# Segment-recurrent attention beside a gated MLP on one core: work of GpSimd given to VectorE and ScalarE, and a new order of all tasks

## The chip, the cores and the metric

The kernel runs on one core of one Trainium2 chip. A core has five engines that run side by side and meet only at semaphores: TensorE (PE, matrix multiplication into the accumulation memory PSUM), VectorE (DVE), ScalarE (ACT), GpSimd (POOL) and SyncE (SP, which here only issues transfers). The metric is the device time of one execution in microseconds, as the median of several runs. Beside it there is one profiled execution, with a record for each instruction; its span runs from the first to the last record.

## The reference

Input is one sequence x of 2048 tokens by 512 features, in bf16. Two branches are computed and mixed token by token:

```python
g = sigmoid((x * gate_w).sum(-1))            # one number per token
a = attention(x, wq, wk, wv, wo, beta)       # branch A
h = gelu(x @ w_gate) * (x @ w_up)            # branch B, 1792 wide
b = h @ w_down
out = g * a + (1 - g) * b
```

Branch A has 32 heads of width 16 and works in four segments of 512 tokens. Inside a segment it is causal softmax attention. What came before enters through a memory per head, a 16x16 matrix M and a vector z:

```python
pq = phi(qs)                                 # phi(t) = t + 1 if t > 0, else exp(t)
a_mem = (pq @ M) / (pq @ z + 1e-6)
o = sigmoid(beta) * a_mem + (1 - sigmoid(beta)) * softmax(qs ks^T / 4 + mask) @ vs
pk = phi(ks);  M = M + pk^T @ vs;  z = z + pk.sum over tokens
```

## The kernel before

**An order written out by hand.** The kernel does not loop over its stages in the order in which they run. It first declares 1,364 tasks (class `Task`, `Sched.add`), each with a function that emits a few instructions, and then `Sched.run` goes through one long string, `ORDER`, word by word, and emits each task's instructions. Each engine executes its own instructions strictly in that order. A word is a task's name, then where needed `@A`, `@D`, `@P` or `@S` (the engine that takes it: ScalarE, VectorE, GpSimd or SyncE; without it the first engine of the task's list), then `#` and letters that name the buffers it takes. So the string decides the order on each engine, the engine of many small tasks, and which buffer is used again when.

**The tasks of a segment s** (c is one of four chunks of eight heads, pr a pair of chunks, kt and qt a quarter of the segment's 512 tokens, hs one of 14 pieces of the MLP's width):

- `qs.c`, `ks.c`, `vs.kt` are projections, four accumulation steps each, into one PSUM bank ("gen", two of them, letters a and b). `eq`, `ek`, `ev` move the result to SBUF on VectorE or ScalarE.
- `kes.c` and `kos.c` (function `odd_copy`) copy k times a 0/1 column, `even` or `odd`, into kO, so that both heads of a 32-row strip can be taken apart.
- `lgN`, N from 0 to 71, 18 in each segment, holds a block of logits in two of the three double banks "lg" (letters a, b, c). Before the first one, matmuls use the whole array; after it, every matmul is split into four on 32-column groups (`mm4`), and logits use four 32-row groups.
- `exNa`, `exNb` are the exponentials of the two halves, 128x1024 each, on ScalarE; `asNa`, `asNb` zero the masked part on GpSimd (`affine_select`; every ninth slot, "as8", has 64-partition pieces, two a half).
- `pvs.ce`, `pvs.co` (function `pv_group`) multiply the even and odd heads' probabilities with v: 40 matmuls of 64 to 256 columns, whose sequence is that of the list `parts`. `epv` transposes the result on VectorE, and `r`, `rg`, `n`, `m`, `o` normalise, mix with the memory's part and transpose back.
- `E`, `Q`, `Em`, `ph` (function `phi`) compute phi as min(exp(t), 1) + max(t, 0): an exponential on ScalarE, a maximum, a minimum, and an addition. `pks.pr` transposes phi(k) by two DMAs from SP, `Ms.pr` and `eM` add to the memory, `mbd` and `zbd` lay it out, `num`, `den`, `nm`, `rma`, `rmr`, `rmg` read it for the next segment. `bdec` and `wosc` scale a mask and w_o by values of sigmoid(beta), once.
- `gts.hp` and `egt` are the MLP's gate and its gelu (into one lg double bank, on ScalarE), `ups.hs` and `eup` the up projection and the product on VectorE. Going from an exponential to a gelu or back, `act` adds a tiny operation, before which a table load stands.
- `dns.qt.hs` and `wos.qt.c` add both branches' outputs into one bank; `os` scales by 1 - g, `st` stores.
- `zs.kt` reduce x * gate_w, from rows of x that lie in the place of w_down (tile wdn) and w_o until they are done; `zsp` and `g2` finish g. On SP, `lx2`, `lx3` load x of segments 2 and 3 by four DMA transpositions each, `wdn0` to `wdn3` load w_down over the rows that are done, `wo` loads w_o.

A PSUM bank may be written again only when its evacuation is done, so each TensorE task waits for the evacuation of the task two places earlier in the same set of banks, unless that was done long before.

**Lines that the steps touch.** L385 is the split matmul (L381 the undivided one), L683 logits, L743 pv, L858 M; L233 all exponentials and gelus, L231 the tiny operation and its table load; L237 and L239 copies on ScalarE and VectorE; L413 ko, L423 and L425 ke; L556 z; L610 the up product; L622 one step of `eb`; L715 and L710 masks; L760 the pv transposition; L783 m; L810, L813, L817 the maximum, minimum and addition of phi; L958 nm; L1000 and L998 os.

Of the kernel before, what the change touches and what calls it, by code (L numbers as in the profile page):

```python
# [36 lines left out]
k0f1.0 xt0.1 xt1.1 xt2.1 ext0.1 xt3.1 ext1.1 k0f2.0 ext2.1 ext3.1 k0f3.0 k0f0.1 k0f1.1 k0f2.1  # L37
k0f3.1 q0.0#ba ek0.3@A ek0.2@D ek0.1@A ek0.0@D gt0.0#b Ek0.1#a ke0.0@D#a ko0.0@D ke0.2@D#b ke0.3@D
ko0.2@D gt0.1#a Qk0.1#a eq0.0@D egt0.0#a Emk0.1 phk0.1@P#a q0.1#a egt0.1#b lg0#cb eq0.1@D v0.3#b
ko0.1@D q0.2#ab ev0.3@D Ek0.0#a gt0.5#a eq0.2@D ex0a#a Qk0.0#a ke0.1@D ex0b#b as0a gt1.4#c as0b  # L40
gt0.3#b egt0.5#c lx3 gt0.2#a egt0.3#d egt1.4#e q1.0#bc egt0.2#f up0.7#a eq1.0@D lg1#bc eup0.7
v0.1#b z0.1 ex1b#c v0.0#a z1.1 ev0.1@A z1.2 as1b lg2#ac ex1a#d q1.1#b ev0.0@D ex2b#e v0.2#a
eq1.1@D ex2a#f as2b lg3#bc ev0.2@D up0.3#b pk0.1#a tb ex3b#g up1.8#a eup0.3 ex3a#h as1a lg4#ac
eup1.8 v1.0#b as2a ex4b#i up0.11#a ev1.0@D vh0.0@A lg5#bc eup0.11 as4b k1.0#bc ex5b#j z1.3
pv0.0e#aa omg ex4a#k gt0.6#c Emk0.0 phk0.0@D#a ex5a#a vh0.1@D pk0.0#b Eq1.0#a as5a gt1.1#a epv0.0e
as3a ek1.0@D as4a as3b gt0.4#b z1.0 egt0.6#g Qq1.0#a wdn1 Emq1.0 egt1.1#h lx2 eb phq1.0@P#a
pv0.0o#a up0.13#b egt0.4#i epv0.0o lg6#ca eup0.13 k1.1#a bde0@P bde3@D z0.0 M0.0#b ex6b#b gt1.5#b
eM0.0 z3.2 ex6a#c ek1.1@D as6b M0.1#b Ek1.0#a as6a lg7#ac eM0.1 z0.2 v1.1#a ex7a#d z2.2 v1.2#b
z2.0 ex7b#g gt1.2#a bde1@D Emk1.0 z0.3 z2.3 wdn0 gt1.3#c z3.1 egt1.5#j z3.3 ev1.1@A z3.0 gt1.6#b
egt1.3#k z2.1 ev1.2@D wdn2 zsp2 egt1.2#l zbd0 up0.5#a egt1.6#m as5b up1.11#b eup0.5 pv0.1e#ab  # L50
eup1.11 lg8#ca ko0.3@D up0.10#b epv0.1e ex8a#h Qk1.0#a up0.1#a ke1.0@A#a eup0.10 as8a ex8b#i as7a
lg9#bc eup0.1 as7b up1.2#b ex9a#k as8b zsp1 pv0.1o#a ex9b#a eup1.2 lg10#ab epv0.1o q0.3#b ex10a#b
r0.0#a phk1.0@D#a up1.9#a eq0.3@A as10a r0.1#b pk1.0#b ex10b#c zsp0 lg11#ca eup1.9 v1.3#b ex11a#j
mbd0.0 zsp3 up0.0#a ev1.3@D ex11b#d as11a lg12#bc wo eup0.0 g2 q1.2#ba wdn3 ex12b#e q1.3#a eq1.2@D
ex12a#f as9b lg13#ac as10b eq1.3@D up0.6#b as9a ex13b#g as11b up1.3#a ex13a#h eup0.6 lg14#bc
eup1.3 Eq1.1#a gt2.2#a mbd0.1 ke1.1@D ex14b#i Qq1.1#a Emq1.1 phq1.1@D#b k2.0#ba rg0.1 den1#aa
gt1.0#c eden1 egt2.2#n ek2.0@D rma1.0#a bde2@D up1.10#a wos1@D egt1.0#o n0.1#a as12a up0.8#b
eup1.10 as13b rma1.1 pv0.2e#ab eup0.8 lg15#ac ex14a#a epv0.2e up2.4#b as12b rma1.2 ex15a#b up1.0#a
eup2.4 ex15b#c lg16#ba eup1.0 as13a up0.4#b rma1.3 ex16b#k pv0.2o#a eup0.4 lg17#ca ex16a#e epv0.2o
ko1.0@P k1.2#bb rmr1 ex17a#f num1.1#aa gt2.0#b r0.2#b as14a ek1.2@A rg0.2 as15a enum1.1 ex17b#g  # L60
as16a rmg1 rg0.0 gt2.3#c n0.2#b nm1.1@P#a as14b egt2.0#p gt2.1#a as17a as15b egt2.3#q as17b as16b
pv0.3e#bb egt2.1#r k1.3#a epv0.3e ke1.2@D#b lg18#bc ek1.3@D up0.2#b ex18b#h up1.1#a eup0.2 ex18a#a
ko1.1@D lg19#ac mbd0.3 up0.12#b eup1.1 ex19b#b as18a pv0.3o#a as18b eup0.12 ex19a#c lg20#bc wos2@D
epv0.3o up1.5#b ex20b#i up0.9#a eup1.5 ex20a#d ko1.3@D lg21#ac mbd0.2 up1.12#b eup0.9 ex21b#e
as20a r0.3#b v2.3#a ex21a#f eup1.12 lg22#bc ev2.3@D up2.5#b ex22a#g as20b up1.6#a ex22b#j eup2.5
o0.1 lg23#ab Ek1.1#a gt2.4#c eup1.6 as22b as21b ex23a#k Qk1.1#a as22a o0.2 as19b up2.2#b n0.0#a
as21a rg0.3 num1.0#aa gt2.6#a as19a vh1.1@D egt2.4#s vh1.0@A omz gt2.5#c enum1.0 egt2.6#t eup2.2
pv1.0e#aa n0.3#b egt2.5#u q2.0#bb Emk1.1 epv1.0e phk1.1@P#a lg24#ac eq2.0@D pv1.0o#a up1.4#b
ex24b#a epv1.0o r1.0#a nm1.0@P#b pk1.1#a q2.1#a ke1.3@A eup1.4 ex24a#b as23a num1.2#ba eq2.1@D
ex23b#c lg25#ca enum1.2 up1.13#a ex25b#h o0.0 as23b k2.1#b nm1.2@P#c eup1.13 ex25a#e wos0@D  # L70
lg26#ba up1.7#a ek2.1@D ex26a#f as25a as24a M1.0#b as25b eup1.7 ex26b#g lg27#cb as24b eM1.0 as26a
M1.1#a rg1.0 ex27b#j pv1.1e#bb as26b eM1.1 ko1.2@D wos3@P pv1.1o#a epv1.1e ex27a#a lg28#ab epv1.1o
up2.13#b ex28b#b as27a k2.2#ac as27b eup2.13 ex28a#c as28b n1.0#a lg29#cb ek2.2@A up2.3#b mbd1.1
ex29a#k up2.7#a eup2.3 ex29b#d as29a lg30#ac eup2.7 up2.8#b ex30b#e o0.3 zbd1 ex30a#f lg31#bc
as29b eup2.8 up2.10#a ex31b#g r1.1#b v2.2#b eup2.10 ex31a#h lg32#ac ev2.2@D as28a up2.0#a ex32a#i
as30b as30a pv1.2e#ba eup2.0 as31b Eq2.0#a as31a lg33#ba epv1.2e q3.0#ac m1.0@P ex32b#a k2.3#b
eq3.0@D ex33b#b as32b rg1.1 Qq2.0#a up2.1#a ex33a#c ek2.3@D as33b as32a lg34#ca eup2.1 pv1.2o#b
# [6 lines left out]
ex36b#d dn0.0.2 dn0.0.3 dn0.0.4 wo0.3.3 dn0.0.5 lg39#ac as36b dn0.0.6 os0.3@D#a ex39a#e dn0.0.7
as37b dn0.0.8 dn0.0.9 dn0.0.10 ex39b#f dn0.0.11 as39a dn0.0.12 num1.3#ba as37a dn0.0.13 wo0.0.0
enum1.3 as38b vh2.0@A wo0.0.1 wo0.0.2 wo0.0.3 o1.0 lg40#ba os0.0@A#b q2.2#ba n1.2#a ex40b#g st0.0
q2.3#a eq2.2@A Qq3.0#a phq3.0@D#a lg41#ca eq2.3@A pv2.0e#ba r1.3#b Eq2.1#a m1.2@D dn0.2.0#a
dn0.2.1 rg1.3 dn0.2.2 nm1.3@D#b dn0.2.3 ex40a#j dn0.2.4 dn0.2.5 mbd1.3 dn0.2.6 Qq2.1#a dn0.2.7
epv2.0e dn0.2.8 ex41b#k dn0.2.9 as40a dn0.2.10 o1.2 dn0.2.11 dn0.2.12 ex41a#a dn0.2.13 Emq2.1
# [1004 lines left out]
```

## Time and profile before

| quantity | value |
|---|---|
| median of 3 runs | 270.41 us (269.59 to 271.2) |
| the profiled execution's own time | 270.36 us |
| its span | 268.6 us |
| granted TensorE clock | 1.00 |
| VectorE busy | 182.7 us, 68% |
| ScalarE busy | 222.0 us, 83% |
| GpSimd busy | 142.7 us, 53% |
| exponentials L233 | 144 x 1029 ns, 137.7 us busy |
| table loads L231 | 20 x 1283 ns, 25.7 us |
| GpSimd additions of phi L817 | 4, 2128 and 2137 ns |
| the same on VectorE | 8, 676 and 730 ns |
| ko L413 | 2 on GpSimd, 1565 ns; 14 on VectorE, 403 ns |
| Q L810 on VectorE | 12, 419 and 449 ns |
| E L233 on ScalarE | 12, about 1058 ns |

The busy time of an engine is the time in which at least one of its records is open; records that follow each other overlap by some 0.1 us, so sums of the mean durations are larger. A matmul's record lasts longer than the time that it keeps the array (379 ns for 512 columns), and records of up to four column groups run side by side, so TensorE's pace is read from the distance between starts, not from a record's length. "Idle before" names what ended an engine's wait. The chain of waits goes back from the last instruction to whatever released each step; its pieces are given as start, length and what ran.

### The profile page before, as it was taken

Reading aid. Unit: us, or ns where it says so; the run is one execution under the profiler, and the core shown is the slowest. Engines: PE = TensorE matmul, PEld = TensorE weight load, DVE = VectorE, ACT = ScalarE, POOL = GpSimd, SP = SyncE. Lnnn points to the kernel's source line nnn. Section 1 sums busy time; section 2 is a strip of 40 time slices with the busy share of each in tenths; the row PEclk is TensorE's granted clock in tenths of the full one; section 3 lists DMA queues with packets and bytes.
Section 4 is the critical chain, followed back from the end, with each engine's and each line's share of the span. In section 5 each row is a group of like instructions: output and inputs, shape, how many; then the busy total and the mean of one; then the engine's idle time right before and its main releaser. Section 6 shows DMA issues by size and latency. Waiting matters only on the chain.

```text
span 268.6 us, 13714 instructions
## 1 busy us (share of the span) xinstructions
PE 262.6 (98%) x6276; PEld 143.5 (53%) x6276; DVE 182.7 (68%) x367; ACT 222.0 (83%) x260; POOL 142.7 (53%) x262
## 2 busy tenths in 40 slices
...
GB/s 208 370 242 307 171 45 159 101 83 43 120 2 5 2 2 2 45 2 5 2 4 44 22 2 19 68 5 2 43 5 2 2 2 5 61 4 8 58 51 52
DMA packets 23610, 15.96 MB, mean 59 GB/s; under 512 B 13824, under 2 KB 22528, under 8 KB 23552
## 3 DMA queue, kind: packets, MB, share of 16 engines
...
q8 instruction: 49, 0.80, 1.3%
q10 hardware_dynamic: 1152, 0.92, 1.0%
...
HBM read 9.84 MB, written 2.10 MB: 44 GB/s over the span
## 4 chain that ended last, share of the span: by engine, by line
PE 88%; ACT 5%; DVE 4%; issue 1%
PE dn L385 23%; PE up L385 18%; PE gt L385 14%; PE lg L683 8%; PE pv L743 7%; PE v L385 5%; PE q L385 4%; PE k L385 4%; PE k L381 2%; ACT pT L233 2%; ACT L231 1%; ACT G L233 1%; PE num L385 1%; PE warm L381 1%; DVE ebr L622 1%; DVE G L610 1%
## 5 line engine op out<-in xcount | busy, mean ns | idle before, releaser
L233 ACT ACTIVATE pT<-lg 128x1024 bf16<-128x1024 f32 x144 | 137.7, 1029 | 11.1 <-PE lg L683 7.4
L715 POOL TENSOR_SCALAR_AFFINE_SELECT pT<-pT 128x256 bf16<-128x256 bf16 x128 | 52.5, 436 | 61.9 <-ACT pT L233 60.3
L385 PE MATMUL dn<-wdn,G 128*32 128x512 bf16 (+1 forms) x952 | 57.0, 367 | 0.0
L385 PE MATMUL up<-xT,wup 128*32 128x512 bf16 x896 | 56.6, 380 | 0.0
L610 DVE TENSOR_TENSOR G<-up,G 128x512 bf16<-128x512 f32 x56 | 38.5, 687 | 19.8 <-PE up L385 19.0
L385 PE MATMUL gt<-xT,wga 128*32 128x512 bf16 x832 | 48.0, 379 | 0.1
L710 POOL TENSOR_SCALAR_AFFINE_SELECT pT<-pT 64x1024 bf16<-64x1024 bf16 x32 | 37.1, 1160 | 16.5 <-ACT pT L233 11.0
L760 DVE STREAM_TRANSPOSE T<-pv 128x512 f32<-128x512 f32 x32 | 22.7, 711 | 17.8 <-PE pv L743 17.7
L385 PEld LDWEIGHTS <-wga 128*32 128x32 bf16 x832 | 23.4, 97 | 20.7 <-issue 0.4
L385 PEld LDWEIGHTS <-G 128*32 128x32 bf16 x952 | 23.9, 97 | 19.4
L385 PEld LDWEIGHTS <-wup 128*32 128x32 bf16 x896 | 22.9, 96 | 19.4 <-issue 0.2
L233 ACT ACTIVATE G<-gt 128x1024 bf16<-128x1024 f32 x28 | 27.5, 1016 | 3.4 <-PE gt L385 3.3
L231 ACT ACT_TABLE_LOAD x20 | 25.7, 1283 | 0.4
L743 PE MATMUL pv<-pT,vz 128*32 128x256 bf16 (+2 forms) x768 | 22.5, 238 | 0.1
L998 ACT ACTIVATE osb<-dn,omz 128x512 bf16<-128x512 f32 (+1 forms) x6 | 3.7, 616 | 20.8 <-PE dn L385 20.8
L743 PEld LDWEIGHTS <-vz 128*32 128x32 bf16 x768 | 17.2, 97 | 5.8 <-issue 0.6
L385 PEld LDWEIGHTS <-xT 128*32 128x32 bf16 x528 | 13.4, 96 | 12.2 <-DVE xT L786 0.2
L385 PE MATMUL dn<-wo,xT 128*32 128x512 bf16 (+1 forms) x272 | 19.1, 367 | 0.0
L923 POOL TENSOR_SCALAR rm<-Tm 32x32 f32<-32x32 f32 x48 | 15.1, 315 | 7.3 <-DVE Tm L917 4.2
L683 PEld LDWEIGHTS <-kO 32*128 32x128 bf16 x640 | 9.7, 92 | 15.7 <-issue 14.9
L743 PE MATMUL pv<-pT,vh 128*32 128x64 bf16 x512 | 17.6, 193 | 0.0
L683 PE MATMUL lg<-qT,kO 32*128 32x64 bf16 (+2 forms) x640 | 16.9, 217 | 0.5 <-issue 0.5
...
## 6 DMA issues: line engine op xcount, KB each, us to landing
...
```

Source lines behind the costliest of these rows:

```text
L231: nc.scalar.activation(nil[0][:, 1:2], nil[0][:, 0:1], func)
L233: nc.scalar.activation(dst, src, func, **kw)
L381: nc.tensor.matmul(out, lhsT=lhsT, rhs=rhs, start=start, stop=stop)
L385: nc.tensor.matmul(out[a], lhsT=lhsT[:, a], rhs=rhs, start=start, stop=stop, tile_position=(0, 32 * j), skip_group_check=True)
L610: UPT[(s, hs)] = evac("DVE", g, box, lambda e, t: nc.vector.tensor_mul(G[(s, hs // 2)][:, hs % 2, :], t[:, :], G[(s, hs // 2)][:, hs % 2, ...
L683: nc.tensor.matmul(A[j // 2][:, j % 2, at:at + n], lhsT=l, rhs=q[a, i, q0:q0 + n], start=True, stop=True, tile_position=(32 * j, 0))
L710: nc.gpsimd.affine_select(out=v, in_=v, pattern=[[0, 16], [1, HB]], compare_op=ALU.is_ge, fill=0.0, base=0, channel_multiplier=-1)
L715: nc.gpsimd.affine_select(out=v, in_=v, pattern=[[0, 4], [1, HB]], compare_op=ALU.is_ge, fill=0.0, base=HB, channel_multiplier=-1)
L743: nc.tensor.matmul(t[32 * j:32 * j + 32, q0:q0 + n], lhsT=v, rhs=pT[(s, u, j // 2)][:, j % 2, at:at + n], start=(n_ == 0), stop=(n_ == len ...
L760: nc.vector.transpose(TT[key][:, e, :, :].rearrange("p a b -> p (a b)"), t[:, :])
L923: eng_of[e].tensor_scalar_add(RMt[s][32 * j:32 * j + 32, c, :, :], bx["Td"][32 * c:32 * c + 32, :, 2 * j:2 * j + 2], 1e-6)
L998: nc.scalar.activation(bx["o"][:, lo:hi], box["t"][:, 0:hi - lo], AF.Copy, scale=g)
```

## The change

No operation of the computation changes, with one exception in kind: a maximum with zero may be a ReLU. What changes is which engine takes what, the sequence inside pv, and the whole order.

1. **Engine lists.** A helper `scaled` multiplies by a per-partition column on ScalarE or another engine. `ko`, `bde` and `wos` may go to VectorE or ScalarE (before: VectorE or GpSimd). Q of phi may go to VectorE or ScalarE (before: VectorE). The addition `ph` is for VectorE alone (before: GpSimd or VectorE). `m` and `nm` keep VectorE or GpSimd.
2. **pv.** The ten parts of a pv group are no longer sorted by quarter; they go in the sequence `PVO`, in which long and short pieces alternate at first.
3. **ORDER** is replaced as a whole: which task stands where on each engine, which engine takes it, and which buffer.

By the two orders, tasks per engine move so (before to after): GpSimd `ph` 4 to 0, `ko` 2 to 0, `wos` 1 to 0, `bde` 1 to 0, `nm` 6 to 5, `m` 5 to 7; ScalarE `ko` 0 to 5, `Q` 0 to 1, `bde` 0 to 1, `ek` 7 to 5, `eq` 4 to 3, `ev` 3 to 2, `ke` 4 to 2, `vh` 4 to 2, `os` 6 to 4; VectorE takes the rest (`ph` 8 to 12, `ko` 14 to 11, `wos` 3 to 4, `vh` 4 to 6, `ke` 12 to 14, `ek` 9 to 11, `os` 11 to 13, `Q` 12 to 11, `m` 7 to 5, `nm` 6 to 7).

```diff
+    def scaled(e, dst, src, f):
+        if e == "ACT":
+            nc.scalar.activation(dst, src, AF.Copy, scale=f)
+        else:
+            eng_of[e].tensor_scalar_mul(dst, src, f)
...
-            eng_of[e].tensor_scalar_mul(
-                QK[ko][:, c % 2, :, HB:],
-                QK[("k", s, pr)][:, c % 2, :].rearrange("p (k n) -> p k n", n=P), odd[:, :])
+            scaled(e, QK[ko][:, c % 2, :, HB:],
+                   QK[("k", s, pr)][:, c % 2, :].rearrange("p (k n) -> p k n", n=P), odd[:, :])
...
-        EVQK[("o", s, c)] = add(f"ko{s}.{c}", ["DVE", "POOL"], fo, kind="ko",
+        EVQK[("o", s, c)] = add(f"ko{s}.{c}", ["DVE", "ACT"], fo, kind="ko",
...
+    PVO = (0, 1, 2, 5, 3, 6, 4, 7, 8, 9)
...
-            parts.sort()
+            parts = [parts[x] for x in PVO]
...
-        def f_q(_):
+        def f_q(e):
             box["Q"] = rtile("Q1", [P, 2, L])
-            nc.vector.tensor_scalar_max(box["Q"][:, :, :], src()[:, :, :], 0.0)
+            if e == "ACT":
+                nc.scalar.activation(box["Q"][:, :, :], src()[:, :, :], AF.Relu)
+            else:
+                nc.vector.tensor_scalar_max(box["Q"][:, :, :], src()[:, :, :], 0.0)
...
-        q = add("Q" + name, "DVE", f_q, kind="Q", deps=[e], alloc=["Q1"], frees=[free])
+        q = add("Q" + name, ["DVE", "ACT"], f_q, kind="Q", deps=[e], alloc=["Q1"], frees=[free])
...
-        return add("ph" + name, ["POOL", "DVE"], f_a, kind="ph", deps=[m, q], alloc=[ring],
+        return add("ph" + name, ["DVE"], f_a, kind="ph", deps=[m, q], alloc=[ring],
```

`bde` and `wos` change in the same way as `ko`. Of ORDER, four places, before and after. The beginning:

```diff
-egt1.4#e q1.0#bc egt0.2#f up0.7#a eq1.0@D lg1#bc eup0.7
-v0.1#b z0.1 ex1b#c v0.0#a z1.1 ev0.1@A z1.2 as1b lg2#ac ex1a#d q1.1#b ev0.0@D ex2b#e v0.2#a
+lx2 egt0.0#c gt1.4#b egt0.5#d ev1.1@A gt0.2#c egt1.4#e eq0.3@A z0.3 v0.1#a egt0.2#f Qk0.0@D#a
+Emk0.0 q1.0#bc ev0.1@D lg1#ab eq1.0@D up0.7#a ex1b#c z1.0 v0.0#b ko0.1@D eup0.7 ex1a#d as1b lg2#cb
```

The place near lg6 (before), with `eb` and a phi addition on GpSimd:

```diff
-as3a ek1.0@D as4a as3b gt0.4#b z1.0 egt0.6#g Qq1.0#a wdn1 Emq1.0 egt1.1#h lx2 eb phq1.0@P#a
-pv0.0o#a up0.13#b egt0.4#i epv0.0o lg6#ca eup0.13 k1.1#a bde0@P bde3@D z0.0 M0.0#b ex6b#b gt1.5#b
+pv0.0o#b egt1.1#i Emq1.0 lg6#ca epv0.0o up0.13#a z0.1 k1.1#b z3.0 ex6a#b phq1.0#a gt1.5#b ek1.1@D
+ex6b#c eup0.13 M0.1#b Ek1.0#a as6b lg7#ca eM0.1 as6a z2.0 v1.2#a ex7a#d omg pv0.1e#bb ex7b#g eb
```

The stretch from lg26 to lg29:

```diff
-lg26#ba up1.7#a ek2.1@D ex26a#f as25a as24a M1.0#b as25b eup1.7 ex26b#g lg27#cb as24b eM1.0 as26a
-M1.1#a rg1.0 ex27b#j pv1.1e#bb as26b eM1.1 ko1.2@D wos3@P pv1.1o#a epv1.1e ex27a#a lg28#ab epv1.1o
-up2.13#b ex28b#b as27a k2.2#ac as27b eup2.13 ex28a#c as28b n1.0#a lg29#cb ek2.2@A up2.3#b mbd1.1
+q2.1#b as24b enum1.2 ex25a#e lg26#bc eq2.1@D k2.2#ac ke2.0@D#a ex26a#f pv1.1e#bb ek2.2@D ex26b#g
+lg27#ab as26a epv1.1e up2.13#a as25b ex27b#k nm1.2@D#c up1.7#b rg1.0 eup2.13 ex27a#a as27b lg28#cb
+eup1.7 as25a up1.13#a as26b ex28a#b n1.0#b as27a pv1.1o#b eup1.13 ex28b#c m1.0@P lg29#ac epv1.1o
```

The end:

```diff
-dn3.3h1.12 os2.3@D#b dn3.3h1.13 st3.0@A wo3.3h1.0 wo3.3h1.1 wo3.3h1.2 wo3.3h1.3 os3.3h1@A st2.3
-st3.3h1@A
+dn3.3h1.11 dn3.3h1.12 dn3.0.12 st3.3h0@A dn3.0.13 wo3.0.0 st3.2@A wo3.0.1 wo3.0.2 wo3.0.3
+dn3.3h1.13 wo3.3h1.0 wo3.3h1.1 os3.0@D#b wo3.3h1.2 wo3.3h1.3 os3.3h1@A st3.0@S st3.3h1@A
```

On SP the order of the loads was lx3, pk0.1, pk0.0, wdn1, lx2, wdn0, wdn2, pk1.0, wo, wdn3; it is lx2, pk0.1, pk0.0, wdn0, wdn3, lx3, wdn2, pk1.0, wdn1, wo, where wdn3 needs every z to be done. M1.0 stood next to lg27 and stands next to lg20; M1.1 stood behind lg27 and stands ahead of lg25.

More of the change, by code (lines that the diff above doesn't have):

```diff
@@ L36 @@
 warm#a warm.free open#babcaab xt0.0 xt1.0 xt2.0 ext0.0 xt3.0 ext1.0 fill ext2.0 ext3.0 k0f0.0
[L37 to L77, printed above, removed]
@@ L84 @@
[L84 to L89, printed above, removed]
@@ new lines @@
+Emk0.0 q1.0#bc ev0.1@D lg1#ab eq1.0@D up0.7#a ex1b#c z1.0 v0.0#b ko0.1@D eup0.7 ex1a#d as1b lg2#cb
+ev0.0@D up1.8#a ex2b#e as1a z2.1 q1.1#b pk0.1#a tb eup1.8 ex2a#f as2b lg3#ab eq1.1@A v1.0#a ex3b#g
+v0.2#b ev1.0@D as2a ex3a#h lg4#cb ev0.2@D up0.3#a ex4b#i phk0.0#a gt0.4#a ex4a#j vh0.1@D Eq1.0#a
+pk0.0#b vh0.0@D lg5#bc up0.11#b eup0.3 ex5b#k z1.3 pv0.0e#aa as5b gt0.6#c ex5a#a epv0.0e as4a
+Qq1.0@D#a eup0.11 as5a as3b k1.0#ac z3.1 as3a egt0.6#g gt1.1#b ek1.0@D as4b z1.1 egt0.4#h z3.3
+pv0.0o#b egt1.1#i Emq1.0 lg6#ca epv0.0o up0.13#a z0.1 k1.1#b z3.0 ex6a#b phq1.0#a gt1.5#b ek1.1@D
@@ new lines @@
+ex6b#c eup0.13 M0.1#b Ek1.0#a as6b lg7#ca eM0.1 as6a z2.0 v1.2#a ex7a#d omg pv0.1e#bb ex7b#g eb
+gt1.6#c z0.2 z2.2 Qk1.0@D#a gt1.3#a z0.0 egt1.6#j z3.2 wdn0 egt1.5#k epv0.1e gt1.2#c z1.2 egt1.3#l
+Emk1.0 ev1.2@D up0.8#b ko0.2@D egt1.2#m z2.3 up0.5#a eup0.8 bde2@A wdn3 zsp2 lx3 lg8#ba eup0.5
+up1.11#b bde0@D ex8b#h up0.10#a eup1.11 ex8a#i as8b lg9#ca eup0.10 as7b up1.2#b as7a ex9a#j
+phk1.0#a as8a up1.9#a eup1.2 ex9b#a zsp1 lg10#bc eup1.9 pv0.1o#b ex10b#b wdn2 zsp0 v1.3#a epv0.1o
+pk1.0#a ex10a#c as10b lg11#ac ev1.3@D zsp3 q1.2#bb ex11a#k up1.3#a as9a g2 eq1.2@D as11a ex11b#d
@@ new lines @@
+wdn1 lg12#ba eup1.3 wo q1.3#b ex12a#e up0.1#a eq1.3@D ex12b#f as9b r0.1#a lg13#cb as10a eup0.1
+M0.0#b as11b ex13b#g gt2.2#a r0.0#b rg0.1 ex13a#h Eq1.1#a lg14#bc as12a eM0.0 up0.0#a wos3@D
+ex14b#i ke1.0@D#a zbd0 up1.10#b Qq1.1@D#a rg0.0 n0.1#a as14b gt1.0#c bde3@D as12b eup1.10 as13b
+egt2.2#n eup0.0 as13a pv0.2e#bb wos2@D egt1.0#o Emq1.1 up0.6#a epv0.2e lg15#ac eup0.6 pv0.2o#b
+wos0@D up2.4#a epv0.2o ex14a#a up1.0#b eup2.4 ex15a#b as14a r0.2#a up0.4#a ko1.1@D ex15b#c rg0.2
+eup1.0 lg16#ba eup0.4 k2.0#ba ex16a#j mbd0.0 n0.2#b gt2.0#c ex16b#e phq1.1#b bde1@D ke1.1@A
@@ new lines @@
+lg23#bc eup2.2 up0.12#a ex23a#j rmg1 as19b mbd0.3 up2.5#b as18b ex22b#k nm1.1@D#a as22a gt2.6#b
+eup2.5 as21a o0.2 as22b as21b rg0.3 num1.0#ba vh1.1@D egt2.6#s gt2.5#a Emk1.1 n0.0#b Qk1.1@A#a
+ke1.3@D eup0.12 gt2.4#b ko1.3@A enum1.0 egt2.5#t phk1.1#a nm1.0@P#b pv1.0e#aa o0.1 pk1.1#b
+egt2.4#u pv1.0o#b epv1.0e as23a lg24#ab epv1.0o up1.12#a o0.0 up1.4#b ex24a#a eup1.12 v2.3#a
+ex23b#b eup1.4 as24a r1.0#b M1.1#b ex24b#c ev2.3@D as23b lg25#ac eM1.1 num1.2#aa n0.3#a ex25b#h
+q2.1#b as24b enum1.2 ex25a#e lg26#bc eq2.1@D k2.2#ac ke2.0@D#a ex26a#f pv1.1e#bb ek2.2@D ex26b#g
@@ L645 @@
     t_eb = add("eb", "DVE", f_eb, kind="eb", deps=[t_om])
-    t_bde = [add(f"bde{c}", ["DVE", "POOL"], lambda e, c=c: f_bde(e, c), kind="bde", deps=[t_eb])
+    t_bde = [add(f"bde{c}", ["DVE", "ACT"], lambda e, c=c: f_bde(e, c), kind="bde", deps=[t_eb])
              for c in range(NCH)]
-    t_wo = [add(f"wos{c}", ["DVE", "POOL"], lambda e, c=c: f_wo(e, c), kind="wos",
+    t_wo = [add(f"wos{c}", ["DVE", "ACT"], lambda e, c=c: f_wo(e, c), kind="wos",
                 deps=[t_om, TAB["wo"]]) for c in range(NCH)]
```

153 lines of the change are left out of this document (86 added, 67 removed).

## The prediction

> **What bounds the kernel now.** I read the busy shares first, then the chain of waits, then the time lines of the engines wherever the chain breaks.
>
> ```profile
> span 268.6 us, 13714 instructions
> ...
> PE 262.6 (98%) x6276; PEld 143.5 (53%) x6276; DVE 182.7 (68%) x367; ACT 222.0 (83%) x260; POOL 142.7 (53%) x262
> ...
> q8 instruction: 49, 0.80, 1.3%
> ```
>
> TensorE is busy all the time, and its granted clock is 1.00, but a busy PE may still hide short waits. So I compared its pace with the pace of undisturbed pieces on the chain:
>
> ```profile
> 49.10 5.18 PE gt L385 x96
> ...
> 62.04 0.86 PE up L385 x16
> 62.90 0.34 PE lg L683 x32
> 63.25 0.98 PE v L385 x16
> 64.22 0.86 PE up L385 x16
> 65.09 0.33 PE lg L683 x12
> 65.42 1.84 PE q L385 x32
> ```
>
> Four matmuls of 512 columns on the four column groups take 0.216 us (5.18/24). Thirty-two take 1.84 between two logit tasks and 1.73 elsewhere, so each of the 72 logit tasks costs 0.11 for the change of tiling. The work at this pace: 885 sets of four (3540 records) x 0.216 = 191.2; 24 undivided matmuls x 0.216 = 5.2; 36 sets of 256 columns x 0.109 = 3.9; 32 pv x 0.56 = 17.9; 72 lg x 0.33 = 23.9; 6 M x 0.23 = 1.4; 72 changes x 0.11 = 7.9; the start to the last first-segment k matmul 8.3. Together 259.7. The stream runs from 1.04 to 265.05, 264.0 long, so **about 4.3 us are waits**, and nothing else can be won on TensorE: both programs hold the same 6276 matmuls and 72 logit tasks. Three kinds of wait:
>
> ```profile
> 119.32 0.28 PE lg L683 x23
> 119.60 0.49 issue
> 120.09 0.26 PE lg L683 x9
> ...
> 123.50 0.60 PE lg L683 x10
> ```
>
> First, "issue": lg29 takes 1.03 instead of 0.34, lg31 0.60 instead of 0.33, and pv2.1o, near 170, 0.78 instead of 0.56: 0.69 + 0.27 + 0.22 = 1.18 us with no engine to wait for. Queue q8 moved 49 blocks; TensorE's 12,552 instructions (a weight load and a matmul each) make 256 a block. Counted along TensorE's pace, the order before puts 512 instructions into 5.7 us just ahead of lg29; its next densest places hold 512 in about 6.8 (the approach to the same spot), 7.6 and 8.0 us. I read these waits as instructions that arrive too late.
>
> ```profile
> 40.70 0.17 DVE L621 RECIPROCAL ebr<-omg 128x4 f32<-128x4 f32 x1
> 40.91 2.12 DVE L622 TENSOR_SCALAR ebr<-ebr 128x4 f32<-128x4 f32 x1
> 42.95 0.70 DVE L760 STREAM_TRANSPOSE T<-pv 128x512 f32<-128x512 f32 x1
> ...
> 40.87 2.13 POOL L817 TENSOR_TENSOR pq<-E,Q 128x1024 bf16<-128x1024 bf16 x1 [1.31 <-DVE ebr L621]
> ...
> 43.70 1.05 PE L385 MATMUL k<-xT,wk 128*32 128x512 bf16 x16 [0.37 <-DVE T L760]
> ```
>
> Second, GpSimd holds VectorE up: an operation on four columns lasts exactly as long as the POOL addition beside it, the pv transposition behind it is late, and k1.1 waits for its bank: 0.44 us lost (lg6 takes 0.77 to the next start).
>
> Third, ScalarE. Between lg18 and lg27 (89.0 to 115.0, 26.0 us) it never rests long:
>
> ```profile
> 88.76 1.28 ACT L231 ACT_TABLE_LOAD   x1
> 90.05 0.20 ACT L231 ACTIVATE nil<-nil 128x1 f32<-128x1 f32 x1
> 90.16 7.50 ACT L233 ACTIVATE pT<-lg 128x1024 bf16<-128x1024 f32 x8
> ```
>
> An exponential costs (7.50-1.03)/7 = 0.92 in a row, a change between exponentials and gelu about 1.5. Its work in this stretch (18 exponentials, 3 gelus, an E, a vh, a ke, 3 changes) is 25.9 us against 25.4 of TensorE work: here ScalarE sets the pace. The remaining waits (gt0.5 0.31, lg25 0.31, M1.1 0.29, pv2.1e 0.30, M2.1 0.20, up0.8 0.21, up1.4 0.17, and smaller) are buffers that ScalarE or VectorE frees late.
>
> **The change part by part.** Sums stand against the profiled execution's 270.36 (span 268.6 plus 1.76 around it); the median is 270.41, 0.05 above.
>
> *Spread of instructions.* Along the same pace the new order's densest place holds 512 instructions in 7.6 us (near lg24) and 384 in 5.25; M1.0, which stood beside M1.1 and two pv groups, goes to lg20. Bounds: -1.18 if all three places heal, 0 if the wait moves. The densest place is nearest to those that pass today (512 in 8.0 near 207 without a wait, though 7.6 near 159 precedes the 0.22): I take **-1.1**.
>
> *GpSimd.* Off POOL go four phi additions (2.13 each), two ko (1.57), a wos (1.67), a bde (0.61), and one nm (1.22); two m (1.16) come on: about -12 us of 142.7. No long POOL addition is left beside ebr: **-0.44**. Still there are the 32 halves of as8 (1.16) and seven m, which held up VectorE in other places (a ke near 142 took 1.23), so the kind of wait is not gone.
>
> *VectorE* gets four phi additions (about 0.6 in a row), and by my count of both orders 2 ek, 2 ke, 1 eq, 1 ev, 2 vh, 2 os, 1 nm, 1 wos, and gives 3 ko, 2 m, 1 Q: +6.6 us on 161 in a row. Its densest stretch (lg18 to lg27) holds 20.9 us in 24.9, so TensorE's work covers it. Where cover fails, the price is on the page: the phi addition of 0.91 us ahead of an up evacuation at 165 made pv2.1e wait 0.30. Eight additions on VectorE made one such wait, so four more make 0.15; bounds 0 and 4 x 0.30 = 1.2. Against it stand the DVE waits named above, of which the new order undoes some (up0.8, M2.1 stand elsewhere). Together **-0.3**, bounds -0.7 and +0.9.
>
> *ScalarE* gets 5 ko, a Q as ReLU and a bde. A 128x512 ko there lies between the 128x256 ke (0.40 in a row) and E (0.95): I take 0.73. The Q is nearest to E: 0.95. That is +4.9; it gives 2 ek, 1 eq, 1 ev (0.48 each), 2 ke (0.40), 2 vh (0.95), 2 os (0.59), -5.8. The 20 changes of table stay. Net -0.9 in all, but between lg18 and lg27 a Q and a ko replace a vh and a ke: 26.2 us against 24.9 of TensorE. TensorE cannot pass this stretch without having lost 1.3 us by then; it has lost 2.1 by lg27 now, so the floor allows the terms above. Cost **0**, bounds 0 and +0.5.
> The Trainium skill, page "ScalarE: Activation LUTs", section "Rules for kernel authors", puts ReLU, max and multiplication on VectorE. The rows agree (Q 0.45 there, E 1.06 here). By that rule the moves cost 4.9 us on the engine that paces this stretch, unless the returned work pays for it; that outcome is the second case below.
>
> *Order within pv* (PVO). Same 40 matmuls; they run at 0.56 (1280 columns at 512 per 0.216 are 0.54), and eight sets of 34 columns in M take 0.23, so short sets hide their loads in any order: 0, bounds -0.3 and +0.3 over all 32.
>
> *SP.* lx2 goes ahead of lx3 and the w_down pieces change places; wdn3 waits for every z and holds lx3, wdn2, wdn1 and wo behind it. First needs: x2 at 67 us (its four transpositions landed by 33 for the tensor in that place), x3 at 126, w_down at 132. Those are covered: 0. Tight is pk1.1: gt2.6 ends at 101.3 by pace, 102.7 with ScalarE's lateness; its gelu (0.2 + 1.0), Qk1.1, now on ScalarE (0.95), phk1.1 (0.7) and two transpositions (3.8 from the first issue to the last landing today) end at 109.4, and M1.1 is due at 109.1 by pace, 110.6 with today's 1.5 of waits. Slack 1.2 us; gone if TensorE gets ahead of ScalarE there, when it costs up to 0.3: a bound only.
>
> *First 30 us.* The gate_w row: z0.3 now heads VectorE's queue before Qk0.0, Emk0.0, ev0.1, eq1.0. Issued at 16.0, landed 9.4 later:
>
> ```profile
> L321 SPq DMA_DIRECT2D wdn<-in_gate_w_dram x1: 499/499/499, 16.0 to 16.0; - x1
> ```
>
> So VectorE is released at 25.4 and eq1.0 ends 2.6 later, at 28.0; v0.0 needs its bank at 28.0 by pace, about 28.4 with the waits of today. Cost 0, slack 0.3. The last store follows the last matmul as before, now beside a 128 KB store: 0, +-0.2.
>
> Sum: -1.1 - 0.44 - 0.3 = -1.8: 270.36 - 1.8 = **268.6 us**, with 2.5 us of waits left.
>
> **The rivals.**
> *ScalarE keeps its lateness*: lg18 to lg27 starts as late as today (1.5 us behind the pace at lg18) and loses 26.2 - 24.9 = 1.3 more; TensorE is 2.8 behind at lg27, not 2.1, and the later issue waits alone are saved: -1.18 + 0.7 - 0.2 elsewhere = -0.7: 269.7. For it: 26.2 against 24.9. Against: three logit buffers let TensorE arrive late without waiting.
> *The change does not thin the stream enough*: the issue wait moves to lg24 or stays near pv2.1o; -0.44 - 0.3 = 269.6. For it: 512 in 7.6 us beside a place that waits today. Against: all places at 8.0 and above pass.
> *The gate_w row lands late*, slower: VectorE sits at z0.3, and lg1, up0.7, v0.0 and with them the exponentials stand. It decides from a landing at 25.7; each us after that costs one. Behind the row, 512 KB of x rows land every 1.5 us; if it falls behind three of them (30 us) the price is 4.3 less slack taken up later, 1.8 already won: about 271.8. Against: the queue ahead of it is unchanged.
>
> **How the numbers follow.** Forecast 268.6: 0.60; ScalarE 0.20; stream 0.11; gate_w 0.09. Below: all bounds at their good end and only ScalarE's 1.3 and a start of 0.4 left is 4.3 - 1.7 = 2.6 won, 267.7, less 0.2 for the store. Above: the rivals at 269.7 with 0.4 of VectorE waits, 270.1. Range **267.5 to 270.1**; the gate_w case and some of the rest stay out. About 0.5% (1.35 us) is what a measurement of this kernel tells from no change: faster means under 269.06. Forecast 0.56 of its 0.60, a fifth of the ScalarE case and some of the stream case: 0.63; same 0.28; slower 0.09.
>
> **What would show it.** Right: lg29, lg31 and pv2.1o at 0.34, 0.33, 0.56 with no "issue" piece over 0.2 on the chain; ebr under 0.3 us; k1.1 not waiting for T; no L817 on POOL; about 261.7 us from the first matmul to the end of the last. Wrong: issue pieces near lg24 to lg26; exponentials that start with their logits long done and lg tasks waiting for L233 between lg18 and lg27; a z instruction at 25 us that ends late with TensorE waiting for eq1.0 or ev0.1; pv over 0.56.

## The result, and the profile after

The changed kernel takes 272.06 us in the median of 14 runs (270.98 to 273.9), beside 270.36 for 14 runs of the kernel before (269.59 to 271.2): a ratio of 1.0063, interval 1.0044 to 1.0081. It is slower by 1.7 us; the forecast was 1.8 us faster. The profiled execution of the changed kernel is one of its longer runs (273.49 us), so its waits are at the upper end of what a run shows.

The page's span, busy times and shares of the chain by engine:

```profile
span 271.4 us, 13732 instructions
...
PE 262.1 (97%) x6276; PEld 143.1 (53%) x6276; DVE 184.1 (68%) x377; ACT 221.1 (81%) x257; POOL 129.4 (48%) x255
...
PE 79%; DMA 9%; SPq 5%; DVE 4%; issue 1%; ACT 1%; ACTq 0%; DVEq 0%
```

TensorE is as busy as before, GpSimd 13 us less, VectorE 1.4 more. New is the last line: 9% of the chain that ended last are transfers and 5% the queue that issues them. The chain in order of time (start, length, what) says which:

```profile
17.45 9.64 DMA wdn<-in_gate_w_dram
27.11 0.70 DVE wdn L557 x2
28.49 0.61 DVE vz L238
29.14 1.05 PE up L390 x16
...
34.17 4.38 DMA pk<-pkT
38.68 0.70 DVE pkT L822
39.40 0.46 DVE vh L238
...
69.36 5.97 DMA wo<-in_A_wo_dram
75.36 0.35 DVE wo L244
...
77.30 0.69 DVE G L611
78.04 0.74 PE pv L745 x40
```

Three times in this chain TensorE's work hangs on a transfer by way of a VectorE instruction that stands ahead of an evacuation. (Lines of the changed kernel lie between one line earlier and five further on than before: L390 the split matmul, L685 logits, L745 pv, L611 the up product, L557 z, L822 the phi addition, L232 exponentials, L236 and L238 copies; L244 is the multiplication in `scaled`.) The time lines of VectorE and ScalarE give the idle time ahead of each such instruction, in brackets, with what ended it:

```profile
27.11 0.69 DVE L557 SCALAR_TENSOR_TENSOR wdn<-wdn 128x512 bf16<-128x512 bf16 x1 [9.10 <-DMA wdn<-in_gate_w_dram]
...
33.27 0.23 ACT L232 ACTIVATE tbh<-beta 128x32 f32<-128x32 bf16 x1 [0.77 <-DMA beta<-in_A_beta_dram]
...
38.68 0.69 DVE L822 TENSOR_TENSOR pkT<-E,Q 128x1024 bf16<-128x1024 bf16 x1 [1.94 <-DMA pk<-pkT]
...
75.36 0.35 DVE L244 TENSOR_SCALAR wo<-wo,omg 128x512 bf16<-128x512 bf16 x1 [3.23 <-DMA wo<-in_A_wo_dram]
```

Four heads of queues: z0.3 waits for the row of gate_w, tb for beta, phk0.0 for its buffer, which the transposition pk0.1 is still reading, and wos3 for w_o. The matmul tasks behind them, from the first matmul to that of the next task, take: lg1 0.74 instead of 0.33, v1.0 1.45 instead of 0.87, up0.11 1.74 instead of 0.87, gt1.0 3.46 instead of 1.73: 3.6 us together. A fifth wait, 1.1 us for the first piece of w_gate near 11 us (q0.0 takes 1.93 instead of 0.86), has the same loads ahead of it as in the kernel before, where it is absent.

How far TensorE is behind its own pace (the start of a task less the sum of undisturbed lengths ahead of it, worked out from the traces, us):

```
            lg0   lg1   lg6   lg13  lg15  lg18  lg27  lg31  lg54  last task
before      0.39  0.71  0.71  1.26  1.48  1.47  2.08  3.08  4.26  4.4
after       1.58  1.62  3.50  3.51  5.34  5.73  6.55  6.55  6.81  7.2
```

From lg27 to the end the kernel before loses 2.3 us and the new one 0.6. Most of what the new order gives stands there (the rest is gt0.5's 0.31 behind lg0 and lg6's 0.44), and all of it and more is spent before lg18: the new order loses 1.6 by lg0, where the kernel before had lost 0.4, 1.9 from lg1 to lg6, and 1.8 from lg13 to lg15. The waits that the prediction named are gone; first lines of the same chain, then the answer on the tile ebr:

```profile
123.45 0.34 PE lg L685 x32
123.79 1.84 PE up L390 x32
125.63 0.33 PE lg L685 x12
...
127.81 0.33 PE lg L685 x12
```

```profile
L623 DVE TENSOR_SCALAR ebr<-ebr x1: 170/170/170, 52.7 to 52.7; 128x4 f32<-128x4 f32 x1
```

lg29 (at 123.45) and lg31 (at 127.81) take 0.34 and 0.33; ebr takes 170 ns, not 2124.

### The profile page after: what moved, and what is told of

Its sections match the earlier page's. It is cut to its first block, busy times and chain, and to the rows that moved or that the text cites. A ratio compares the mean times of both kernels' runs of the same rounds, so it can differ in the third digit from the quotient of the medians.

```text
span 271.4 us, 13732 instructions
## 1 busy us (share of the span) xinstructions
PE 262.1 (97%) x6276; PEld 143.1 (53%) x6276; DVE 184.1 (68%) x377; ACT 221.1 (81%) x257; POOL 129.4 (48%) x255
## 4 chain that ended last, share of the span: by engine, by line
PE 79%; DMA 9%; SPq 5%; DVE 4%; issue 1%; ACT 1%; ACTq 0%; DVEq 0%
PE dn L390 23%; PE up L390 16%; PE gt L390 12%; PE lg L685 8%; PE pv L745 7%; PE k L390 4%; SPq L300 4%; PE v L390 4%; DMA wdn<-in_gate_w_dram 4%; PE q L390 3%; DMA wo<-in_A_wo_dram 2%; DMA wdn<-in_A_x_dram 2%; DMA pk<-pkT 2%; PE num L390 1%; SPq L851 1%
## 5 line engine op out<-in xcount | busy, mean ns | idle before, releaser
L232 ACT ACTIVATE pT<-lg 128x1024 bf16<-128x1024 f32 x144 | 137.5, 1027 | 12.0 <-PE lg L685 9.2
L717 POOL TENSOR_SCALAR_AFFINE_SELECT pT<-pT 128x256 bf16<-128x256 bf16 x128 | 53.3, 442 | 85.9 <-ACT pT L232 77.4
L390 PE MATMUL dn<-wdn,G 128*32 128x512 bf16 (+1 forms) x952 | 57.4, 367 | 0.0
L390 PE MATMUL up<-xT,wup 128*32 128x512 bf16 x896 | 56.0, 380 | 0.4 <-DVE vz L238 0.3
L390 PE MATMUL gt<-xT,wga 128*32 128x512 bf16 x864 | 50.2, 379 | 0.0
L611 DVE TENSOR_TENSOR G<-up,G 128x512 bf16<-128x512 f32 x56 | 38.4, 687 | 14.1 <-PE up L390 10.6
L390 PEld LDWEIGHTS <-wga 128*32 128x32 bf16 x864 | 23.9, 97 | 21.5 <-DMA wga<-in_B_w_gate_dram 0.4
L390 PEld LDWEIGHTS <-G 128*32 128x32 bf16 x952 | 24.6, 97 | 18.9
L390 PEld LDWEIGHTS <-wup 128*32 128x32 bf16 x896 | 22.2, 96 | 20.8 <-issue 1.0
L232 ACT ACTIVATE G<-gt 128x1024 bf16<-128x1024 f32 x28 | 27.7, 1016 | 3.6 <-PE gt L390 3.3
L230 ACT ACT_TABLE_LOAD x20 | 25.7, 1283 | 0.3
L745 PE MATMUL pv<-pT,vz 128*32 128x256 bf16 (+2 forms) x768 | 20.8, 238 | 2.3 <-DVE G L611 2.3
L745 PEld LDWEIGHTS <-vz 128*32 128x32 bf16 x768 | 16.5, 97 | 8.5 <-DVE G L611 2.1
L390 PEld LDWEIGHTS <-xT 128*32 128x32 bf16 x528 | 13.9, 96 | 12.2 <-issue 0.9
L1003 ACT ACTIVATE osb<-dn,omz 128x512 bf16<-128x512 f32 (+1 forms) x4 | 2.3, 580 | 21.9 <-PE dn L390 21.4
L1005 DVE TENSOR_SCALAR osb<-dn,omz 128x512 bf16<-128x512 f32 x13 | 9.7, 746 | 13.5 <-PE dn L390 13.3
L390 PE MATMUL dn<-wo,xT 128*32 128x512 bf16 (+1 forms) x272 | 18.0, 367 | 0.0
L390 PE MATMUL v<-wv,xT 128*32 128x512 bf16 x256 | 16.7, 380 | 0.5 <-ACT qT L236 0.4
L685 PEld LDWEIGHTS <-kO 32*128 32x128 bf16 x640 | 9.5, 93 | 14.2 <-issue 13.2
L685 PE MATMUL lg<-qT,kO 32*128 32x64 bf16 (+2 forms) x640 | 16.1, 217 | 0.0
```

The costliest lines, as they stand in the source:

```text
L230: nc.scalar.activation(nil[0][:, 1:2], nil[0][:, 0:1], func)
L232: nc.scalar.activation(dst, src, func, **kw)
L390: nc.tensor.matmul(out[a], lhsT=lhsT[:, a], rhs=rhs, start=start, stop=stop, tile_position=(0, 32 * j), skip_group_check=True)
L611: UPT[(s, hs)] = evac("DVE", g, box, lambda e, t: nc.vector.tensor_mul(G[(s, hs // 2)][:, hs % 2, :], t[:, :], G[(s, hs // 2)][:, hs % 2, ...
L685: nc.tensor.matmul(A[j // 2][:, j % 2, at:at + n], lhsT=l, rhs=q[a, i, q0:q0 + n], start=True, stop=True, tile_position=(32 * j, 0))
L717: nc.gpsimd.affine_select(out=v, in_=v, pattern=[[0, 4], [1, HB]], compare_op=ALU.is_ge, fill=0.0, base=HB, channel_multiplier=-1)
```

## The experiments

Theory H: the loss is waits for transfers at the heads of in-order queues. Rival S: another engine, ScalarE first, would take the time back. The first four kernels take the waits away, one group at a time and then together. Moved words are shown with their old and new neighbours.

**e1.**

```diff
-... up0.0#a wos3@D ex14b#i ...
+... pv0.2e#bb wos2@D wos3@D egt1.0#o ...
```

> The changed kernel with wos3 moved eight VectorE tasks further back, behind wos2, so that the wait for w_o (landed at 75.0 in the profiled run, VectorE idle for 3.23 us at the head of its queue) holds up nothing. Theory H (the loss is waits for transfers at the heads of in-order queues, four of them): gt1.0 goes from 3.46 to about 1.73, and the time falls by 1.4 to 1.75, from 272.06 to 270.3 to 270.7, a ratio to the kernel before of 1.000 to 1.002. Rival S (ScalarE or another engine sets the pace from 66 to 90 us and would take the time back): gt1.0 heals, but waits of the same size appear at the next logits or up tasks; the time falls by under 0.6.

Measured: 270.47 us, ratio 1.0005 (0.9988 to 1.0021); 1.6 less than the changed kernel. gt1.0 takes 1.73. As H said.

**e2.**

```diff
-... bde2@A wdn3 zsp2 lx3 ... wdn2 ... pk1.0#a ... wdn1 ... wo
+... bde2@A wo wdn3 zsp2 lx3 ... wdn2 ... pk1.0#a ... wdn1 ...
```

> The changed kernel with wos3 left where it is and the load of w_o put three loads and a transposition further forward on SP, ahead of wdn3 and lx3. Theory H: w_o lands near 62 to 66 instead of 75, the 3.23 us of idle VectorE are gone, and the time falls by 1.4 to 1.75, as in the run beside it, since the same wait is taken away from its other end. Rival S: under 0.6. If this one heals and the other does not, the load order is the cause and not the place in the queue; if only the other heals, w_o was late for another reason than its place on SP.

Measured: 269.55 us, ratio 0.9967 (0.9945 to 0.9990). w_o lands at 60.5 instead of 75.3 and gt1.0 takes 1.73. The gain of 2.5 is more than H said and more than the wait that vanished; e5 below did not repeat the lead of 0.9 over e1.

**e3.**

```diff
-lx2 egt0.0#c ... eq0.3@A z0.3 v0.1#a ... eup0.7 ex1a#d ... q1.1#b pk0.1#a tb eup1.8 ... ex4b#i phk0.0#a
+pk0.1#a lx2 egt0.0#c ... eq0.3@A v0.1#a ... eup0.7 z0.3 ex1a#d ... q1.1#b eup1.8 ... ex4b#i tb phk0.0#a
```

> The changed kernel with three early waits for transfers taken from the heads of their queues: z0.3 behind eup0.7 on VectorE, tb behind ex4b on ScalarE, and pk0.1 ahead of lx2 on SP, so that phk0.0 finds its buffer free. Theory H: lg1 0.33, v1.0 0.87, up0.11 0.87 (0.74, 1.45 and 1.74 in the profiled run, 1.88 us together); the time falls by 0.8 to 1.9, the smaller where an ordinary run has its first loads sooner than the profiled one, to 270.2 to 271.3, and the runs scatter less. gt1.0 stays at 3.4. Rival S: below 0.5. Beside it, the landing of the first piece of w_gate (11.9 against 9.5 in the kernel before, with the same loads ahead of it) shows whether the wait of 1.07 behind q0.0 belongs to the new order: then it is there again; if it is chance, it is gone.

Measured: 270.74 us, ratio 1.0029 (1.0008 to 1.0050); 1.3 less than the changed kernel. lg1, v1.0 and up0.11 take 0.33, 0.87 and 0.87, gt1.0 3.43. The wait for the first piece of w_gate is there again, 0.8 us. The runs scatter as much as those of the changed kernel (269.85 to 272.77), so that part of the expectation was a miss.

**e4**, e1 and e3 together.

> Both: the three early places of e3 and wos3 of e1. Theory H: the gains add up, 2.3 to 3.6 in all, and what is left is the new order as it was predicted without late transfers: 268.4 to 269.7, a ratio to the kernel before of 0.993 to 0.9975. Rival S: 270.5 to 271.5, since TensorE runs into ScalarE as soon as it is less late.

Measured: 269.11 us, ratio 0.9948 (0.9930 to 0.9966). The gains add up (1.6 of e1 and 1.3 of e3 make 2.9; measured 2.95): S is refuted.

**e5**, the opening of e3 and the early w_o of e2.

> The three early places of e3 and the earlier w_o load of e2, nothing of e1. Theory H (heads of queues): the gains of e3 (-1.3) and e2 (-2.5) add up, as e1 and e3 did in e4: 268.2 to 268.9, a ratio to the kernel before of 0.991 to 0.995; this is the forecast of 268.6 for the change without late transfers. Rival (e2's lead of 0.9 over e1 is scatter of the first loads): 269.1 as e4, 0.9955.

Measured: 269.30 us, ratio 0.9940 (0.9920 to 0.9960). That is e4 again, within both intervals, and not e2 + e3. The traces agree: from the start of lg1 to the start of the last matmul e4 and e5 both take 235.65 us, so the two ways to take away the wait for w_o are worth the same. e2's lead over e1 is put down to the scatter of the first loads, though no run settles it.

What the landings say across the profiles of the changed order (times of the trace, us; the last four columns are lengths of tasks, undisturbed 0.33, 0.87, 0.87, 1.73):

```
        w_gate, 1st piece  gate_w row   w_o    lg1   v1.0  up0.11  gt1.0
after        12.2            27.1      75.3   0.74  1.45   1.74    3.46
e1           10.3            23.3      72.6   0.33  0.87   1.33    1.73
e2           10.9            25.9      60.5   0.70  1.41   1.69    1.73
e3           11.4            25.9      72.7   0.33  0.87   0.87    3.43
e4           12.2            26.7      73.6   0.33  0.87   0.87    1.73
```

e1 and e2 have the opening of the changed kernel untouched. Where the row landed at 23.3, lg1 and v1.0 did not wait at all and up0.11 lost 0.45; where it landed at 25.9 they lost 0.37, 0.54 and 0.82. So the early three depend on when a run's first loads come in; gt1.0 does not.

**e6.** The kernel before with its four phi additions on GpSimd moved to VectorE in place (`phk0.1`, `phq1.0`, `phk1.1`, `phq2.1`: `@P` becomes `@D`).

> The kernel before with nothing changed but the four phi additions of GpSimd, which go to VectorE at the same places. The prediction took 0.44 us for the end of the long GpSimd addition beside ebr, and gave back 0.15 for four more additions on VectorE. Theory L (a VectorE operation on a few columns stands still beside the GpSimd addition): ebr falls from 2.12 to under 0.3, k1.1 no longer waits, lg6 takes 0.33 instead of 0.77; the time falls by 0.2 to 0.45, to 269.9 to 270.2 (0.9985 to 0.9995). Rival: 0.6 more on VectorE at each of four places costs as much as is won, 0 to +0.3.

Measured: 269.76 us, ratio 0.9967 (0.9947 to 0.9987): a gain of 0.9 us, twice the upper end of what was expected. VectorE's time line:

```profile
41.23 0.17 DVE L621 RECIPROCAL ebr<-omg 128x4 f32<-128x4 f32 x1
41.43 0.17 DVE L622 TENSOR_SCALAR ebr<-ebr 128x4 f32<-128x4 f32 x1
41.51 0.68 DVE L817 TENSOR_TENSOR pq<-E,Q 128x1024 bf16<-128x1024 bf16 x1
```

ebr takes 0.17 with no GpSimd addition beside it and lg6 0.33: that VectorE's operation stood still beside the addition is shown, and so is its price of 0.44 us. The addition phk1.1, now ahead of an evacuation, makes TensorE wait 0.35 after pv1.0o, the kind of cost that the prediction put down for VectorE. And lg29 takes 0.34 although nothing in TensorE's order was changed. That is most of the surplus (0.44 + 0.69 - 0.35 = 0.78), and the expectation had not named it; theory I below has to explain it.

**e7.** The kernel before with M1.0 and up1.12 exchanged.

```diff
-mbd0.2 up1.12#b eup0.9 ... eup1.12 lg22#bc ... as24a M1.0#b as25b eup1.7 ... lg27#cb as24b eM1.0
+mbd0.2 M1.0#b eup0.9 ... eM1.0 lg22#bc ... as24a up1.12#b as25b eup1.7 ... lg27#cb as24b eup1.12
```

> The kernel before with M1.0 and up1.12 exchanged, so that 512 TensorE instructions near 111 take 7.1 us of TensorE's pace instead of 5.7; all else stays. Theory I (lg29 and lg31 wait for instructions that are fetched too late after a dense stretch): lg29 falls from 1.03 to 0.35 to 0.55 and lg31 from 0.60 to 0.33 to 0.45 with no issue piece at 119; pv2.1o, which has its own dense place near 159, keeps 0.78; the time falls by 0.5 to 0.95, to 269.4 to 269.9 (0.9965 to 0.998). Rival (these are no fetches; the stretch is as long because ScalarE is late there): lg29 heals, but logits tasks nearby wait as much for ScalarE; 270.2 to 270.5.

Measured: 270.81 us, ratio 1.0005 (0.9991 to 1.0019): no gain, where theory I had 0.5 to 0.95. The chain near lg29:

```profile
120.24 0.28 PE lg L683 x23
120.52 0.30 issue
120.83 0.26 PE lg L683 x9
```

lg29 still takes 0.84, and lg31 0.60. M1.0 made a wait of its own: it holds TensorE for 0.23 where the up task held it for 0.86, so v2.3 behind it waited 0.50 for its bank.

**e10**, the other way round: a kernel without the four waits (e8 below) with M1.0 moved back beside M1.1.

```diff
-ex20b#i M1.0#b ek2.1@D ... lg21#ba eM1.0 ... up1.12#a o0.0 up1.4#b ex24a#a ... eup1.4 as24a r1.0#b M1.1#b
+ex20b#i up1.4#b ek2.1@D ... lg21#ba eup1.4 ... up1.12#a o0.0 M1.0#b ex24a#a ... eM1.0 as24a r1.0#b M1.1#b
```

> e8 with M1.0 and up1.4 exchanged, which puts M1.0 beside M1.1 and four pv and logits tasks again: 512 TensorE instructions near 105 take 6.7 us of TensorE's pace, not 7.6, and 256 take 2.5, not 3.5 (5.7 and 1.65 in the kernel before, 7.1 in e7). Theory I (a dense stretch outruns the fetch of instructions): a wait without a releaser of 0.2 to 0.7 appears once between lg25 and lg29, and the time rises by as much, to 268.5 to 269.0. Rival (the waits at lg29 and lg31 hung on where a block of instructions ends in the order before, not on the density): no such wait, 268.1 to 268.5, but for up to 0.3 if M1.0's neighbour waits for VectorE as in e7.

Measured: 269.02 us, ratio 0.9936 (0.9914 to 0.9957), beside 0.9918 (0.9896 to 0.9941) for the same kernel without the exchange, run with it (e11): no difference that the intervals tell. The time is close to what theory I gave, but not by its wait: nothing waits without a releaser between lg25 and lg29. As in e7 the exchange brought a wait for a bank instead, here between M1.0 and v2.3 (from lg1 to the last matmul e10 takes 236.29 us, e11 235.64):

```profile
110.56 1.05 PE L390 MATMUL v<-wv,xT 128*32 128x512 bf16 x16 [0.55 <-DVE G L611]
```

That wait itself thins the stream again, so e10 doesn't decide; with e6 and e7 it leaves density as a poor forecaster. Two other readings of the traces say more. In the kernel before, e6 and e7, pv2.1o breaks off at the same instruction, and lg29 does so in the two of them where it waits; these are instructions 188 and 190 of a block of 256, counted along TensorE's stream, and they start 1.2 to 1.5 us after the nearest 16 KB transfer of queue q8 ended. In e6 that transfer ended at 118.3 and lg29 reached the instruction at 119.8, just 1.5 later: no wait. So lg29 and pv2.1o very likely wait for instructions, by a margin of tenths of a microsecond; it is inferred from these times, since no record names that wait. lg31 breaks off at instruction 76 of a block, and 50 ns after an exponential ends, in all three kernels. Time lines of ScalarE and TensorE in the kernel before:

```profile
122.64 2.85 ACT L233 ACTIVATE pT<-lg 128x1024 bf16<-128x1024 f32 x3 [0.32 <-PE lg L683]
...
123.43 0.67 PE L683 MATMUL lg<-qT,kO 32*128 32x256 bf16 x12
```

Single records put the end of the first of these three exponentials at 123.66 and the restart of lg31 at 123.71, with a matmul that waits for ScalarE's semaphore. lg31 waited for ScalarE to free its second bank.

**e8**, e5 with pv sorted as before.

```diff
-            parts = [parts[x] for x in PVO]
+            parts.sort()
```

> e5 with the parts of a pv group sorted by quarter again, as in the kernel before: the sequence alone is undone. The prediction took 0 for it, bounds -0.3 and +0.3 over all 32 groups: pv stays at 0.56 a group and the time within 0.3 us of e5. A rival: the new sequence lets the weights of short pieces load behind long ones, so that sorted groups take 0.58 to 0.60: +0.6 to +1.3 us.

Measured: 268.30 us, ratio 0.9924 (0.9897 to 0.9951). That is 1.0 below e5, where at most 0.3 was expected, but the ratios' intervals overlap, and the sequence is not the reason. It does nothing to pv itself: the 32 groups take 19.13 us in all in e5 and 19.12 in e8. From lg1 to the last matmul e5 takes 235.65 us, e8 235.71 and its repetition e11 235.64. The whole difference between the profiled runs stands ahead of lg1, where e5 waits 1.2 us for the second piece of w_gate near 16 us and e8 0.1. The profile of e8 shows the four heads gone (shares of the chain, then VectorE near wos3):

```profile
PE 94%; DVE 2%; DMA 2%; issue 1%; ACT 0%; SPq 0%; DVEq 0%
```

```profile
69.24 1.26 DVE L244 TENSOR_SCALAR wo<-wo,omg 128x512 bf16<-128x512 bf16 x1
```

Its lateness (table above, same columns): 0.36, 0.48, 0.70, 0.72, 0.77, 1.16, 1.98, 1.97, 2.23, 2.6.

**e9**, e8 with Qk1.1 and ko1.3 on VectorE.

```diff
-n0.0#b Qk1.1@A#a ke1.3@D eup0.12 gt2.4#b ko1.3@A enum1.0
+n0.0#b Qk1.1@D#a ke1.3@D eup0.12 gt2.4#b ko1.3@D enum1.0
```

> e8 (early places and w_o healed, pv sorted) with Qk1.1 and ko1.3 taken back from ScalarE to VectorE, in the stretch from lg18 to lg27: some 1.7 us less on ScalarE there, 0.8 more on VectorE. Prediction's step (ScalarE costs 0 there, TensorE's waits upstream give it the time): the time stays within 0.2 of e8, 268.1 to 268.5. Rival of the prediction (ScalarE keeps its lateness and sets the pace of this stretch): M1.1 and lg25 stop waiting and the time falls by 0.5 to 1.0, to 267.3 to 267.8. Third: VectorE is the tighter one there, +0.2 to +0.5.

Measured: 269.14 us, ratio 0.9936 (0.9913 to 0.9958), 0.7 above e11 beside it and so outside the 0.2 that was expected, though the intervals overlap. ScalarE is busy for 24.2 us instead of 25.7 between 89 and 115, and that wins nothing: from lg1 to the last matmul e9 takes 235.86 us, 0.2 more than e11, since lg24 waits 0.29 for a transposition on VectorE. The rest of the difference stands ahead of lg1, behind a wait for the second piece of w_gate. The rival is refuted; between the prediction's step and the third case 0.2 us does not decide.

**e11**, e8 again.

> e8 once more, beside e9 and e10, as their measure and to see whether its lead over both kernels holds: theory H has 268.2 to 268.9 and a ratio to the kernel before of 0.990 to 0.995; lg1, v1.0, up0.11 and gt1.0 without waits whenever the first loads land. If the lead of 1.0 over e5 was scatter of the first loads, it lies between the two, near 268.8.

Measured: 268.48 us, ratio 0.9918 (0.9896 to 0.9941). With 0.9924 before, this version is faster than the kernel before by 0.8% and than the changed kernel by some 1.4% (0.992 / 1.0063).

## Why the prediction was wrong

**The step that failed: loads.** The prediction costed SP at 0: "First needs: x2 at 67 us [...], x3 at 126, w_down at 132. Those are covered". It looked for the first matmul that uses each load, and left out w_o, whose first user is a VectorE instruction, wos3. By its own list w_o was now the last of ten transfers on SP, behind wdn3, which waits for every z; it was issued at 69.4 and landed at 75.3, while VectorE reached wos3 at 72.1. In the kernel before w_o was issued at 66.0 and landed at 70.0, and its first user on VectorE ran at 74.2:

```profile
74.20 0.35 DVE L628 TENSOR_SCALAR wo<-wo,omg 128x512 bf16<-128x512 bf16 x1
```

So a cover of 4.2 us became a wait of 3.2, because the load came 5.3 us later and its first user 2.1 us sooner. Price 1.73 us at gt1.0; shown by e1 and e2, which take that wait away from either end.

**The same step for the first 30 us**, "Cost 0, slack 0.3". The row of gate_w was examined, with a landing at 25.4 in one profile; the landings now seen lie between 23.3 and 27.1, so a slack of 0.3 was no cover. Two more heads were not looked for: tb on ScalarE behind beta, and phk0.0 behind the transposition pk0.1, whose place on SP moved behind lx2. In the profiled run the three waits cost 0.41, 0.58 and 0.87; in the median of runs the three together are worth about 1.3 (e3). With both steps put right the forecast would have been 268.6 + 1.7 + 1.3 = 271.6; the 0.4 to the measured 272.06 is not accounted for.

**The rival on the other side** ("The gate_w row lands late", 271.8) came close to the time by chance: its place is one of four, its price 0.4 and not the 1.4 that "each us after that costs one" makes of a landing at 27.1, because TensorE itself was 1.2 us later by lg0 than in the kernel before (1.58 against 0.39), which moved the deadline with it. e2 fits: its row landed 1.2 sooner, TensorE was 1.1 earlier at lg0, and lg1 lost 0.37.

**What held.** Without the four waits the forecast is met: 268.6 was predicted; the kernels without them lie at 269.1 and 269.3 (e4 and e5, with the whole change) and at 268.3 and 268.5 (e8 and e11, with pv sorted), by their ratios 268.2 to 269.0 on the median of 270.41. The sum came out better than its terms, which is luck in part: two of them, ScalarE and VectorE, were off and made up for each other.
- *GpSimd beside ebr*, -0.44: right, by ebr at 0.17 and lg6 at 0.33 in e6 and in the changed kernel.
- *Spread of instructions*, -1.1: the three places healed (1.18 in the trace), but the reason holds for two of them at most. lg31's 0.27 was a wait for ScalarE that I took for "issue". lg29's 0.69 and pv2.1o's 0.22 look like late blocks of instructions; yet a thinner stream left 0.49 of the 0.69 (e7), and an unchanged one lost it all (e6). What times the fetch stays open.
- *ScalarE*, 0, and its rival at 269.7: from lg18 to lg27 the changed kernel lost 0.82 against 0.61 before, a cost of 0.2 within the bounds, not the rival's 1.3; e9 shows that relief there brings nothing. Over the whole kernel the term was a gain: TensorE's waits of 0.1 us and more that end with ScalarE sum to 0.9 in the kernel before (gt0.5, lg25, lg31) and to 0.2 in e4 and e11.
- *Order within pv*, 0: right to 0.01 us of pv's own time, and to 0.1 us from lg1 to the last matmul (e5 against e8 and e11). Medians of whole runs show it only to about 0.5%.
- *VectorE*, -0.3: not measured by itself, and by the traces nearer to 0. TensorE's waits for it of 0.1 us and more, without lg6, sum to 1.4 in the kernel before and to 1.5 and 1.4 in e4 and e11. Gone are up0.8 and M2.1 (0.4 together); new is lg21, 0.29, and lg25, which waited 0.31 for ScalarE, now waits 0.29 in most profiles for an evacuation on VectorE.

Left open is whether and why the runs of the new order scatter more (270.98 to 273.9, against 269.59 to 271.2 beside them; 29 later runs of the kernel before lie between 268.94 and 271.76). The first piece of w_gate landed at 9.8 to 10.6 us in three profiles of the order before and at 10.3 to 12.2 in those of the new one, behind the same loads; too few to call it an effect of the order.
